# Gated mix of two attentions on one core: four value tiles behind the query tiles, sixteen more maxima units in the front, two-step cycles from step 159

## The chip, the cores and the metric

One core of a Trainium2 chip runs the whole kernel; the other cores are idle. The metric is the device time of one execution in microseconds (us). Engines are named as in the profile: PE is TensorE (PEld its weight loads), DVE is VectorE, ACT is ScalarE, POOL is GpSimd, and SP is SyncE, whose queue (SPq) issues every DMA of this kernel.

## The reference

The input `x` is 2048 tokens of 448 numbers. Two attention layers with 16 heads of 28 read it, and a gate per token mixes their outputs:

```python
g = sigmoid((x * gate_w).sum(-1, keepdims=True))
# A: linear attention with learned feature maps
q, k, v = heads(x @ A_wqkv)
phi_q = cat(softmax(q @ w_phi), softmax(-(q @ w_phi)))      # per head, 28 -> 56
phi_k = the same of k
o_A = phi_q @ (phi_k^T @ v) / (phi_q @ sum(phi_k) + 1e-6)
# B: softmax attention over all 2048 keys
p   = softmax(q' @ k'^T * 28**-0.5);  o_B = p @ v'
out = g * (o_A @ A_wo) + (1 - g) * (o_B @ B_wo)
```

Everything is float32. A precise product is made of passes with split numbers: `fp32r` high parts and low parts (`XH`, `XL`), high times high, high times low, low times high.

## The kernel before, in words

**Two parts.** The front (about the first 330 us) makes queries, keys and values of both layers, does all of layer A, and begins layer B. The back (the loop over `s`, 256 steps) does the softmax attention of B.

**Units and steps of B.** Heads come in 4 groups `g` of 4, and queries in 4 blocks `qb` of 512. A pair `gq = 4 g + qb` has 16 steps, one for every 128 keys. In a step the 4 heads' scores are made (`score_group`, line 965, four `st` tiles of 128 keys x 512 queries), ACT takes the exponentials (line 968), and `values` (line 1069) adds `p` times the values into the tile `pv`. The row maximum of every query, which is subtracted inside the score product, must be known before its pair begins: it is loaded into row 0 of the query stack `qst` (`load_nm`).

**Two ways to find the maxima.** In the front, `mx_unit` takes 128 queries x 2 heads x 1024 keys: four matmuls of 28 rows (line 293) into a bank pair `pmb` and a bank pair `pmd`, one ACT `Relu` over `pmd` (line 296), two DVE sums-with-maximum (line 298). A pair `gq` has 16 units. The first `NF` = 44 units are done in the front, so pairs 0 and 1 and three quarters of pair 2. In the back, `mx_visit` does 128 queries x 4 heads x 512 keys: four matmuls (line 330), one ACT pass (line 334), and three DVE reductions and sums (lines 338 and 341), and one more reduction after every fourth visit (line 344). 212 visits do the rest.

**The cycle of steps.** Up to step `TWO` = 191 every step has a visit, and scores are issued as 5 tiles at an even step and 3 at an odd one ("single steps"). From step 191 scores of two steps are issued together at an odd step (8 tiles), both steps' values follow, and only the even step has a visit ("two-step cycles"). So the visits end at step 234 and the maxima of pair 15 are there for step 240.

**Order of the work.** PE, DVE, ACT and POOL run their instructions in the order in which the program writes them; the DMAs on SP are ordered by the scheduler of the framework, and SP issues them one after the other, so that a DMA whose data isn't ready holds up those behind it.

**The front's long loop** runs over `i` from 0 to 42, with `t = i` (16 token tiles for keys and values of A) and `q = i - 16` (16 query tiles of A). For `t` < 16 an iteration does the key tile (`pk`), its features, and the value tile (`pva`); `tick`, called before each of their matmuls, puts units between them at the places in `pace["at"]`. From `q` = 0 on come the query tile `pq`, its features (maxima and minima on DVE, differences on POOL or DVE, exponentials on ACT), the transposes `pft` (`turn`), the numerators `pn` (`numer`), and from `q` = 11 the output tiles of A, `poa` (`out_a`, `out_a2`). The numerators of a block of 256 queries `tb` are divided in four places: `normalize1` copies them to `oUa` and sends the denominators (`dena`) through a DMA; `normalize2` inverts them on DVE and sends them through memory (`rda`) to all partitions (`rsa`); `normalize3`, three iterations later, multiplies on DVE (line 428); `normalize4`, one iteration later, splits the result, ACT high (line 436) and POOL low (line 437); after that `poa` can begin. At `q` = 18 the first tile `vb` of B's values is opened and `value_b` fills it, one tile of 11 matmuls (`pvb`) per iteration, tiles 0 to 7 at `q` = 18 to 25. From `q` = 11 each iteration has one unit.

**PSUM.** There are 8 banks. In the front's pool `ps` three banks rotate for single tiles (tag `s`), with a fourth taken every fourth time (`turn4`), and two bank pairs (tag `mx`) serve `pmb` and `pmd`. After the long loop the pool is closed and opened again with two single banks and three bank pairs (`psn` = 2, 3): two for `pmb`, one for `pmd`.

**The junction.** After the loop the stacks `qst0`, `kst0` to `kst4`, `qst1` are made: a fill with 0 of 128 x 2048 (line 870) and, for keys, a fill of row 0 with -1 (line 872); `qst0`, `kst0` and `kst1` on DVE, the others on POOL. Then queries, maxima and keys are loaded, and value tiles 8 to 14 are made with the 3 units that are left between them, and tile 15 with the scores of step 0.

Of the kernel before, what the change touches and what calls it, by code (L numbers as in the profile page):

```python
# [17 lines left out]
P = 128  # L18
# [11 lines left out]
NF = 44  # L30
# [10 lines left out]
def gated_mix_kernel(ctx, tc, xT, wqkB, wvB, wvA, wkAT, wqAT, phi, woA, woB,  # L41
# [224 lines left out]

    def mx_unit():
# [27 lines left out]
        rl = rlp.tile([P, 2, 512], F32, tag="rl", name=f"rl{u}", bufs=2 if psn[1] == 3 else 1)  # L295
# [6 lines left out]
        if gq == GM and qt == QM - 1:  # L302
            mx_load(g, c)
        if r == 15:
            mx_reduce(gq)
# [247 lines left out]
    po_of = {}  # L553
# [37 lines left out]
    def out_a(t):  # L591
        tb, tl = divmod(t, 2)
        po_of[t] = po = ps_s(f"poa{t}")
        run(po[:, :D], [x for g in range(NG)
                        for x in out_passes(oTs[tb][g // 2], g % 2 * 256 + tl * P, woA_s[:, :, :, :D], g)])
# [151 lines left out]
    def value_b(t, mid=None):  # L747
        pv = ps_s(f"pvb{t}")
        tok_major(pv, t, wvB_s, D, mid)
        nc.scalar.copy(vb[t // 8][:, t % 8, :, 0:DH], pv[:, :D].rearrange("p (h d) -> p h d", d=DH))  # L750
# [12 lines left out]
    for i in range(2 * NT + 11):  # L763
# [4 lines left out]
        if t < NT and t % 2 == 0:  # L768
            mx_unit()
            passes = (55 if t < NT - 4 else 44) + (4 if t >= 4 else 0)  # L770
            pace["n"] = 4 if t >= 4 else 0
            pace["at"] = [passes // 3, 2 * passes // 3] if t in (4, 6, 8) else [passes // 2]
# [13 lines left out]
        if q == 2:  # L786
# [4 lines left out]
            kvT = kv_copy()  # L791
            turn4.append("")
# [15 lines left out]
        if 0 <= t - 1 < NT - 1:  # L808
            fk[t - 1] = features2(fk[t - 1], f"k{t - 1}")
        if q in (0, 1) or q >= 11:  # L810
            mx_unit()
# [41 lines left out]
        if 0 <= q - NT - 2 < 8:  # L853
            value_b(q - NT - 2)
# [12 lines left out]
    def stack(nm, keys):  # L867
        r = at.tile([P, 4, 512], F32R, name=nm)
        eng = nc.vector if nm in ("qst0", "kst0", "kst1") else nc.gpsimd
        eng.memset(f32(r), 0.0)  # L870
        if keys:
            eng.memset(f32(r[0:1]), -1.0)
        return r
# [17 lines left out]
    def load_k(g, kb):  # L891
        kst_of[(g, kb)] = load_stack(kst[(4 * g + kb) % 5], k_d[g], kb * 512, (0, 1, 0, 1))

    NS = NG * NQ * NT
    TWO = 191
# [81 lines left out]
    ps_s_.close()  # L977
    ps = ps_s_.enter_context(tc.tile_pool(name="psv", bufs=1, space=PSUM, reuse_waits="tile"))
    psn[:] = 2, 3
    turn4.clear()  # L980
# [129 lines left out]
    def finish(gq, s):  # L1110
# [26 lines left out]
        d2, d3, d4 = (3, 8, 9) if s < 216 else (2, 5, 5)  # L1137
# [162 lines left out]
```

## Time and profile before

| what | value |
|---|---|
| three runs | 1008.59 us median, 1005.69 to 1008.81 |
| the profiled execution | 1007.98 us, of which the span of the trace is 1006.2 us |
| busy in the span | PE 997.0, ACT 803.4, DVE 679.2, POOL 237.4 us |
| granted clock of TensorE | 0.998 of full speed |
| DMA | 106.23 MB, 106 GB/s on average |
| the long loop's last part, 266 to 311 us | PE 44.70 of 45, DVE 15.42, ACT 22.09 |
| junction, 311 to 334 us | PE 22.58 of 23, DVE 12.52, POOL 14.52, DMA 0.85 |
| single steps, 396 to 600 us | PE 204.00 of 204, ACT 197.56, DVE 167.14 |
| two-step cycles, 823 to 885 us | PE 62.00 of 62, ACT 61.47, DVE 30.05 |

How to read it: the page gives the share of the span in which each engine was busy, then the same in 40 equal slices, then the chain of work that ended last. The end of a matmul is modelled and matmuls overlap, so PE at 99% says that work lay on it nearly all the time, and not that it couldn't go faster. What a stretch really costs is read from the starts of its instructions in the timeline.

### The profile page before, as it was taken

To read this page: it belongs to the slowest core of one execution; us is meant where nothing else is said; L and a number is where in the kernel's file an instruction comes from. 1 tells how busy PE (TensorE), PEld (TensorE's weight loads), DVE (VectorE), ACT (ScalarE), POOL (GpSimd) and SP (SyncE) were. 2 spreads that over 40 slices of the span, in tenths; PEclk is the share of its full clock that TensorE was granted. 3 is DMA by queue.
4 is the path that set the end of the run, shared out by engine and by line. 5 is a ranking of instruction groups with operands and counts; after the bars stand their busy time and mean duration, and the time that the engine had idled before them with its cause. 6 is when DMAs were issued, how large, how long until landed. Compare 5 with 4: busy or idle time off the path is not lost.

```text
span 1006.2 us, 17986 instructions
## 1 busy us (share of the span) xinstructions
PE 997.0 (99%) x6472; PEld 556.3 (55%) x6472; DVE 679.2 (67%) x1340; ACT 803.4 (80%) x1532; POOL 237.4 (24%) x215
## 2 busy tenths in 40 slices
PE   9999999989999999999999999999999999999998
PEld 8878888868888433333333333333333334455656
DVE  5557766997535688888888888888887874544202
ACT  5445545667743899999999999999999999979682
POOL 1265456687436103111011110101201011001010
PEclk9999999999999999999999999999999999999999
DMA  8976313312235703333532123431324345515131
GB/s 296 313 234 212 118 50 108 113 47 82 92 116 137 158 10 84 83 75 77 120 69 75 44 67 86 102 90 49 90 52 97 81 98 145 147 38 148 60 107 55
DMA packets 67769, 106.23 MB, mean 106 GB/s; under 512 B 18368, under 2 KB 28208, under 8 KB 67680
## 3 DMA queue, kind: packets, MB, share of 16 engines
q1 hardware_dynamic: 67680, 105.08, 38.6%
q8 instruction: 51, 0.84, 0.4%
q14 instruction: 38, 0.31, 0.1%
HBM read 73.21 MB, written 31.45 MB: 104 GB/s over the span
## 4 chain that ended last, share of the span: by engine, by line
PE 77%; DVE 0%; ACT 0%; issue 0%
PE st L965 28%; PE pv L1069 25%; PE pm L330 9%; PE poa L117 4%; PE pob L117 3%; PE pvb L135 2%; PE pvb L117 2%; PE pq L117 1%; PE pmb L293 1%; PE pft L533 1%; PE poL L1107 1%; PE pn L547 1%; PE poL L1177 0%; DVE part L341 0%; PE pr L1162 0%; PE pd L1152 0%
## 5 line engine op out<-in xcount | busy, mean ns | idle before, releaser
L968 ACT ACTIVATE p<-st 128x512 f32<-128x512 f32 x1020 | 529.3, 639 | 25.7 <-PE st L965 25.7
L341 DVE TENSOR_REDUCE part<-pm 128x1 f32<-128x512 f32 x477 | 304.7, 685 | 134.8 <-PE pm L330 134.8
L965 PE MATMUL st<-qst,kst 128*128 128x512 f32 x1020 | 303.1, 423 | 0.4 <-DVE acc L1084 0.4
L1069 PE MATMUL pv<-p,vb 128*32 128x512 f32 x2048 | 266.1, 603 | 0.0
L965 PEld LDWEIGHTS st<-qst,kst 128*128 128x128 f32 x1020 | 167.9, 187 | 99.4 <-ACT p L968 48.9
L334 ACT ACTIVATE rl<-pm 128x512 f32<-128x512 f32 x212 | 132.2, 624 | 15.5 <-PE pm L330 13.4
L330 PEld LDWEIGHTS pm<-kc,qc 28*128 28x128 f32 x848 | 40.5, 181 | 177.8 <-issue 104.8
L428 POOL TENSOR_TENSOR oUb<-oUb,rsb 128x512 f32<-128x512 f32 x15 | 19.4, 1291 | 457.0 <-DMA rsb<-rdb 212.2
L338 DVE CUSTOM_DVE_ANT_0 rl<-pm,rl 128x512 f32<-128x512 f32 x159 | 108.2, 681 | 0.0
L330 PE MATMUL pm<-kc,qc 28*128 28x512 f32 x848 | 107.3, 495 | 0.0
L1069 PEld LDWEIGHTS pv<-p,vb 128*32 128x32 f32 x2048 | 45.4, 108 | 94.1 <-issue 87.4
L298 DVE CUSTOM_DVE_ANT_0 rl<-pmb,rl 128x512 f32<-128x512 f32 x88 | 56.6, 681 | 36.9 <-ACT rl L296 36.9
L117 PE MATMUL pqk<-XH,wB 128*128 128x512 f32 x192 | 59.3, 397 | 0.0
L296 ACT ACTIVATE rl<-pmd 128x1024 f32<-128x1024 f32 x44 | 45.4, 1031 | 8.2 <-PE pmd L293 4.5
L623 ACT CAST ev<-pqk 128x512 fp32r<-128x512 f32 x28 | 16.1, 589 | 38.6 <-PE pqk L117 28.8
L117 PE MATMUL poa<-woA_s,oTa 128*128 128x448 f32 x192 | 44.6, 382 | 0.0
L117 PEld LDWEIGHTS pqk<-XH,wB 128*128 128x128 f32 x192 | 35.4, 188 | 8.5 <-issue 1.5
L1084 DVE SCALAR_TENSOR_TENSOR acc<-pob,gate,acc 128x448 f32<-128x448 f32 x12 | 8.2, 681 | 47.2 <-PE pob L117 47.2
L117 PEld LDWEIGHTS poa<-woA_s,oTa 128*128 128x128 f32 x192 | 35.9, 194 | 6.9 <-issue 4.2
L204 POOL TENSOR_TENSOR kc<-kc,kd 28x512 fp32r<-28x512 f32 x12 | 15.4, 1281 | 101.6 <-DMA kc<-qkd 45.8
L624 DVE TENSOR_TENSOR ev<-pqk,ev 128x512 fp32r<-128x512 f32 x28 | 19.1, 690 | 28.8 <-ACT ev L623 28.7
L135 PE MATMUL pva<-wvA_s,XH 128*128 128x450 f32 x128 | 37.6, 371 | 0.0
(163 smaller groups left out, 1175.8 us busy)
## 6 DMA issues: line engine op xcount, KB each, us to landing
qkd<-ev SPq DMA_DIRECT2D x28, 512.0 KB
qst<-qkd SPq DMA_DIRECT2D x64, 224.0 KB
kst<-qkd SPq DMA_DIRECT2D x64, 224.0 KB
od<-oTb SPq DMA_DIRECT2D x48, 112.0 KB
rsa<-rda SPq DMA_DIRECT2D x8, 512.0 KB
rsb<-rdb SPq DMA_DIRECT2D x15, 256.0 KB
kc<-qkd SPq DMA_DIRECT2D x64, 56.0 KB
gad<-ga SPq DMA_DIRECT2D x16, 224.0 KB
```

Of the source, the lines that this page charges most:

```text
L117: nc.tensor.matmul(dst, l, r, start=i == 0, stop=i == len(todo) - 1)
L135: nc.tensor.matmul(dst[:, :n], l, r, start=i == 0, stop=i == len(todo) - 1, skip_group_check=True)
L296: nc.scalar.activation(rl, pd, AF.Relu)
L298: nc.vector.tensor_tensor_reduce(rl[:, i, :], pb[:, i, :], rl[:, i, :], 1.0, LOWEST, ALU.add, ALU.max, part[:, col + i:col + i + 1])
L330: nc.tensor.matmul(pm[j], mxs[("qc", gq)][js, qt * P:(qt + 1) * P], mxs[("kc", g, kb)][js, :], start=True, stop=True, tile_position=(32 * ...
L334: nc.scalar.activation(rl, pm[kb], AF.Relu if kb < 3 else AF.Copy)
L338: nc.vector.tensor_tensor_reduce(r, pm[j], r, 1.0, LOWEST, ALU.add, ALU.max, part[:, col + j:col + j + 1])
L341: nc.vector.tensor_reduce(part[:, col + j:col + j + 1], pm[j], AX.X, ALU.max)
L428: (nc.gpsimd if n == 1 else nc.vector).tensor_mul(oU, oU, rs)
L965: nc.tensor.matmul(st, kst_of[(gq // NQ, kt // 4)][:, j, (kt % 4) * P:(kt % 4 + 1) * P], qst_of[gq][:, j, :], start=True, stop=True)
L968: nc.scalar.activation(p, st, AF.Exp, scale=SCALE)
L1069: nc.tensor.matmul(pv[32 * j:32 * j + 32, :], vb[kt // 8][:, kt % 8, 4 * g + j, :], pt[j], start=kt == 0, stop=kt == NT - 1, tile_position ...
```

## The change

It has six parts.

1. **Four value tiles earlier.** `value_b(0)` to `value_b(3)` run in the iterations `q` = 7 to 10, right behind the query tile's features. Since `vb` isn't open then, they write into two new tiles `early` (`ve`, 128 x 2 x 512 each), whose columns 28 to 31 POOL fills at `q` = 2. At `q` = 18, when `vb` is opened, two DMAs of 512 KB copy them into it. `value_b(4)` to `(7)` run at `q` = 18 to 21; at `q` = 22 to 25 there is no value tile.
2. **Sixteen more units in the front.** `NF` goes from 44 to 60: pairs 0 to 2 and three quarters of pair 3. `pace` gives two places inside every two key and value tiles, not only at `t` = 4, 6, 8 (5 units more); at `q` = 20 and 21 there is a unit inside the value tile (2 more); 12 units stand at the junction and among value tiles 8 to 14, where there were 3. The first visits then belong to head group 0 for four steps only, and group 1's keys are loaded from the last unit on.
3. **Bank pairs.** The pool `ps` is closed and opened with two single banks and three pairs at `q` = 20, not after the loop. The units' work tile `rl` then comes from the tag `rl2`, which the `early` tiles used.
4. **Fills.** All fills of the stacks are on POOL, with one fill of row 0 for `kst0` alone; `kst1` to `kst4` get their row 0 from `kst0` by a DMA of 8 KB each, in `load_k`.
5. **Two-step cycles from step 159.** `TWO` goes from 191 to 159. There are 196 visits in place of 212, and they still end at step 234.
6. **Distances.** The steps of a pair's division in the back (`d2, d3, d4`) are (2, 5, 5) from step 159, not from 216.

```diff
-NF = 44
+NF = 60
@@ mx_unit
-        rl = rlp.tile([P, 2, 512], F32, tag="rl", name=f"rl{u}", bufs=2 if psn[1] == 3 else 1)
+        rl = rlp.tile([P, 2, 512], F32, tag=rlt[0], name=f"rl{u}", bufs=2 if psn[1] == 3 else 1)
...
             mx_load(g, c)
+            if c == NQ - 1 and qb == NQ - 1:
+                mx_load(g + 1, 0)
@@ out_a
-        po_of[t] = po = ps_s(f"poa{t}")
+        po_of[t] = po = po_next.pop() if po_next else ps_s(f"poa{t}")
@@ value_b
-        pv = ps_s(f"pvb{t}")
+        pv = pv_next.pop() if pv_next else ps_s(f"pvb{t}")
         tok_major(pv, t, wvB_s, D, mid)
-        nc.scalar.copy(vb[t // 8][:, t % 8, :, 0:DH], pv[:, :D].rearrange("p (h d) -> p h d", d=DH))
+        v = early[t // 2][:, t % 2] if t < 4 else vb[t // 8][:, t % 8]
+        nc.scalar.copy(v[:, :, 0:DH], pv[:, :D].rearrange("p (h d) -> p h d", d=DH))
@@ the long loop
-            pace["at"] = [passes // 3, 2 * passes // 3] if t in (4, 6, 8) else [passes // 2]
+            pace["at"] = [passes // 3, 2 * passes // 3] 
...
+            early = [ta.tile([P, 2, 512], F32, tag="rl2", name=f"ve{i}", bufs=2) for i in range(2)]
+            early = [e.rearrange("p t (h d) -> p t h d", d=32) for e in early]
+            for e in early:
+                nc.gpsimd.memset(e[:, :, :, 28:], 0.0)
+                nc.gpsimd.memset(e[:, :, :, 28:29], 1.0)
...
+        if 7 <= q < 11:
+            value_b(q - 7)
+        if q == NT + 4:
+            ps_s_.close()
+            ps = ps_s_.enter_context(tc.tile_pool(name="psv", bufs=1, space=PSUM, reuse_waits="tile"))
+            psn[:] = 2, 3
+            turn4.clear()
+            rlp, rlt[0] = ta, "rl2"
+            pv_next.append(ps_s("pvb_next"))
+            po_next.append(ps_s("poa_next"))
...
             vb = [value_tile(0)]
-        if 0 <= q - NT - 2 < 8:
-            value_b(q - NT - 2)
+            for k, e in enumerate(early):
+                nc.sync.dma_start(vb[0][:, 2 * k:2 * k + 2], e)
+        if 0 <= q - NT - 2 < 4:
+            value_b(q - NT + 2, (lambda i: i == 5 and mx_unit()) if q >= NT + 4 else None)
@@ stack
-        eng = nc.vector if nm in ("qst0", "kst0", "kst1") else nc.gpsimd
-        eng.memset(f32(r), 0.0)
-        if keys:
-            eng.memset(f32(r[0:1]), -1.0)
+        nc.gpsimd.memset(f32(r), 0.0)
+        if nm == "kst0":
+            nc.gpsimd.memset(f32(r[0:1]), -1.0)
@@ load_k
+        n = 4 * g + kb
+        if 0 < n < 5:
+            nc.sync.dma_start(f32(kst[n][0:1]), f32(kst[0][0:1]))
+        kst_of[(g, kb)] = load_stack(kst[n % 5], k_d[g], kb * 512, (0, 1, 0, 1))
...
-    TWO = 191
+    TWO = 159
@@ the junction
-    ps_s_.close()
-    ps = ps_s_.enter_context(tc.tile_pool(name="psv", bufs=1, space=PSUM, reuse_waits="tile"))
-    psn[:] = 2, 3
-    turn4.clear()
+    rlt[0] = "rl"
@@ finish
-        d2, d3, d4 = (3, 8, 9) if s < 216 else (2, 5, 5)
+        d2, d3, d4 = (3, 8, 9) if s < TWO else (2, 5, 5)
```

More of the change, by code (lines that the diff above doesn't have):

```diff
@@ L265, in mx_reduce @@
         mxs["fin"].append(reduce)
+    rlt = ["rl"]
     def mx_unit():
@@ L551, in numer @@
         num[tb] = normalize1(ta, pn, f"a{tb}", 2)
-    po_of = {}
+    po_of, po_next, pv_next = {}, [], []
     def load_woA(b):
@@ L891, in load_k @@
     def load_k(g, kb):
-        kst_of[(g, kb)] = load_stack(kst[(4 * g + kb) % 5], k_d[g], kb * 512, (0, 1, 0, 1))
+        n = 4 * g + kb
+        if 0 < n < 5:
+            nc.sync.dma_start(f32(kst[n][0:1]), f32(kst[0][0:1]))
+        kst_of[(g, kb)] = load_stack(kst[n % 5], k_d[g], kb * 512, (0, 1, 0, 1))
     NS = NG * NQ * NT
-    TWO = 191
+    TWO = 159
     slots = {"n": 0}
```

## The prediction

> **What bounds the kernel now.** I read the page first, for what is full.
>
> ```profile
> PE 997.0 (99%) x6472; PEld 556.3 (55%) x6472; DVE 679.2 (67%) x1340; ACT 803.4 (80%) x1532; POOL 237.4 (24%) x215
> ...
> PE 77%; DVE 0%; ACT 0%; issue 0%
> ```
>
> PE is full and the chain of work lies on it, so the time is the sum of what PE issues and of its few gaps. Next the timeline of PE where the back goes from single steps to two-step cycles (columns: start, duration, engine, line, operation, tiles, count):
>
> ```profile
> 817.11 0.51 PE L330 MATMUL pm<-kc,qc 28*128 28x512 f32 x4
> ...
> 819.44 0.50 PE L330 MATMUL pm<-kc,qc 28*128 28x512 f32 x4
> ...
> 822.28 0.51 PE L330 MATMUL pm<-kc,qc 28*128 28x512 f32 x4
> 822.71 2.48 PE L965 MATMUL st<-qst,kst 128*128 128x512 f32 x8
> ...
> 827.41 2.49 PE L965 MATMUL st<-qst,kst 128*128 128x512 f32 x8
> ...
> 832.12 2.22 PE L965 MATMUL st<-qst,kst 128*128 128x512 f32 x8
> ...
> 836.56 2.21 PE L965 MATMUL st<-qst,kst 128*128 128x512 f32 x8
> ```
>
> From 817.11 to 822.28, two steps with two visits take 5.17 us. After 822.71, two steps with one visit take 4.70 the first time, then 4.44 (832.12 to 836.56). The windows give the means:
>
> ```profile
> 750.50:822.80 72.30, 72.30 (x453) 27.79 (x449) 58.83 (x119) 70.14 (x141) 6.37 (x6) 1.00 0.42 95
> 822.80:858.90 36.10, 36.10 (x225) 16.25 (x226) 17.09 (x34) 35.82 (x74) 3.17 (x3) 1.00 0.52 135
> ```
>
> The first is 14 times 5.16 us, the second 8 times 4.51. ACT is at 97% and 99% in them, so ACT is nearly full too; in the front it isn't. The front's only long gap of PE stands ahead of the first output tile:
>
> ```profile
> 215.75 2.70 DVE L428 TENSOR_TENSOR oUa<-oUa,rsa 128x1024 f32<-128x1024 f32 x1 [0.23 <-DMA rsa<-rda]
> ...
> 217.38 0.50 PE L293 MATMUL pmd<-kp,qp 28*128 28x512 f32 x2
> 218.48 1.14 ACT L436 CAST oTa<-oUa 128x512 fp32r<-128x512 f32 x2 [3.58 <-DVE oUa L428]
> 221.00 1.55 PE L547 MATMUL pn<-fT,KV 56*32 56x256 f32 x32 [3.12 <-ACT fT L536]
> ```
>
> ```profile
> 217.90:221.00 3.10, 0.00 (x1) 0.01 (x1) 2.97 (x5) 2.52 (x5) 1.94 (x2) 1.00 0.23 94
> 221.00:226.20 5.20, 5.20 (x45) 3.69 (x46) 5.13 (x11) 3.72 (x6) 5.20 (x5) 0.67 0.15 46
> ```
>
> In the windows the columns are: stretch, length, then busy time and count of PE, PEld, DVE, ACT and POOL, the granted clock, DMA share and GB/s. DVE, full in this stretch, comes late to the first multiplication (L428); ACT waits for it 3.58 us, and the copies of the transposes behind it on ACT are what PE waits for. Then PE runs 5.2 us at a granted clock of 0.67.
>
> **The change, part by part.**
>
> *Back, from step 159 (gain).* 32 steps, or 16 pairs of steps, go from 5.16 to 4.51 us: 16 x 0.65 = 10.4 us less. Bounds: all at 4.44, 11.5 less; all like the first at 4.70, 7.4 less. The shorter distances put the division's wait (DMA of denominators) on DVE 2 steps after the pair's end, 4.5 us; DVE is busy 17.09 of 36.10 there, so I cost it at nothing.
>
> *Sixteen units in the front (loss).* A unit inside a value tile of the junction, and the same tile without one:
>
> ```profile
> 315.41 0.57 PE L135 MATMUL pvb<-wvB_s,XH 128*128 128x448 f32 x2
> ...
> 316.02 0.97 PE L135 MATMUL pvb<-wvB_s,XH 128*128 128x448 f32 x4
> ...
> 319.26 0.56 PE L135 MATMUL pvb<-wvB_s,XH 128*128 128x448 f32 x2
> 319.75 0.50 PE L293 MATMUL pmb<-kp,qp 28*128 28x512 f32 x2
> ...
> 320.50 0.57 PE L135 MATMUL pvb<-wvB_s,XH 128*128 128x448 f32 x2
> ```
>
> Three passes take 0.61 us without and 1.24 with it, so a unit costs 0.63. All sixteen stand inside tiles: 16 x 0.63 = 10.1 us more. Lower bound 16 x 0.50 = 8.0, the busy time alone. So the units moved pay for themselves and no more; what is left decides. Their ACT and DVE work lies beside PE, if the bank pairs come free in time. It is one pass on ACT and two on DVE each, with a short read behind each of the two; and one unit of the profile that took its way through the engines slowly:
>
> ```profile
> L298 DVE CUSTOM_DVE_ANT_0 rl<-pmb,rl 128x512 f32<-128x512 f32 x88 | 56.6, 681 | 36.9 <-ACT rl L296 36.9
> L296 ACT ACTIVATE rl<-pmd 128x1024 f32<-128x1024 f32 x44 | 45.4, 1031 | 8.2 <-PE pmd L293 4.5
> ...
> 129.60 0.50 PE L293 MATMUL pmb<-kp,qp 28*128 28x512 f32 x2
> ...
> 133.18 0.69 DVE L298 CUSTOM_DVE_ANT_0 rl<-pmb,rl 128x512 f32<-128x512 f32 x1
> ```
>
> From the matmuls to the last read it took 4.3 us. With two pairs the next unit must wait for it. At `t` = 12 to 15 the units now follow each other after 16 passes (3.3 us) and 0.5 of their own, 3.8 us: up to 0.5 us late for each of 5. I take 0.6 us in all, between 0 and 2.5. At the junction there are three pairs, and 12 units need 12 x 2 x 0.68 = 16.4 us of DVE in the 23 us that seven tiles and 12 units take on PE (7 x 2.2 + 12 x 0.63): nothing.
>
> *Four value tiles at `q` = 7 to 10 (gain).* PE's work is the same, 11 matmuls each, only moved. But four times 2.2 us (11 x 0.61 / 3) now lie between DVE's late multiplication and PE's need of it, 9 us in place of a lag of 3.1. The gap goes: 3.1 us, and 5.2 x 0.33 = 1.7 us of slow clock, together 4.8 us less. The value tile's copy now stands ahead of the same ACT work, so I leave 0.3 us at the first numerator behind it. Bounds: 4.8 less to 0, if the wait only moves.
> The Trainium skill (TensorE: Matmul & The Clock Gate, Part 1) says that PE falls to half clock after an idle window of about 3.4 us. By that a gap of 3.1 us would cost no clock and the part be worth 3.1 us; the window above shows 0.67 after 3.10 us, and the measurement decides.
>
> *Copies and later value tiles.* The two copies of 512 KB enter the queue at `q` = 18, beside the last denominators. The last block's way in the profile:
>
> ```profile
> 284.91 1.14 SPq L421 DMA_DIRECT2D rda<-dena  x2
> 287.87 0.55 SPq L422 DMA_DIRECT2D rsa<-rda  x1
> ...
> 297.58 1.23 DVE L428 TENSOR_TENSOR oUa<-oUa,rsa 128x1024 f32<-128x1024 f32 x1 [3.13 <-DMA rsa<-rda]
> ...
> 300.59 2.53 POOL L437 TENSOR_TENSOR oTa<-oUa,oTa 128x512 fp32r<-128x512 f32 x2 [8.46 <-ACT oTa L436]
> 302.63 2.73 PE L117 MATMUL poa<-woA_s,oTa 128*128 128x448 f32 x12
> ```
>
> From `rda` to the end of POOL's split it takes 18.2 us (284.91 to 303.12), and poa14 began after 17.7 without waiting, its last passes alone needing the split's end. In the change, between these places stand poa10 to poa13 (4 x 2.7), value tile 7 (2.2) and five units (5 x 0.6), 16 us, since poa12 to poa14 no longer have a value tile each. So PE waits here some 1 us (bounds 0 and 7, below).
>
> *Bank pairs at `q` = 20.* The reopening costs a wait of 0.72 us for ACT's last read:
>
> ```profile
> 311.42 0.50 PE L293 MATMUL pmb<-kp,qp 28*128 28x512 f32 x2 [0.72 <-ACT ga L599]
> ```
>
> It moves from after poa15 to after value tile 5, and unit 39 or poa9 meets it. With the copy out of the value tile in that bank and a unit between them, I count 0.3 less; bounds: nothing less, and 0.7 less.
>
> *Fills.* DVE loses five fills, POOL has seven and one row:
>
> ```profile
> L870 POOL MEMSET kst<- 128x2048 f32 x3 | 5.5, 1825 | 0.0
> L872 POOL MEMSET kst<- 1x2048 f32 x3 | 5.4, 1801 | 0.2
> ...
> kst<-qkd SPq DMA_DIRECT2D x64, 224.0 KB
> ...
> 334.00:336.00 2.00, 2.00 (x16) 1.10 (x17) 1.48 (x3) 1.98 (x5) 0.00 (x0) 1.00 0.93 186
> ```
>
> Eight times 1.8 is 14.5 us on POOL; `kst0`, third in order, is ready after 5.4 us. Scores begin 23 us after poa15, so it costs nothing. Behind the fills stand the DMAs: one query stack and four key stacks of 4 x 224 KB (4.6 MB), and maxima keys and queries of two groups, some 2 MB, of which the second group's now come at steps 1 to 8. At 186 GB/s that is 35 us from about 8 us after poa15 on; the last piece is needed at step 8, some 45 us after it (23 and 8 x 2.6). Nothing, but it is near. The row copies of `kst1` to `kst4` are four more DMAs of 8 KB, behind a fill that is done before them.
>
> **Sum.** -10.4 + 10.1 - 4.8 + 0.3 + 0.6 + 1.0 - 0.3 = -3.5. The profiled execution took 1007.98 us, which gives 1004.5. It lies 0.6 under the median of the three runs (1008.59).
>
> **The rivals.**
> 1. *The last denominators come late (slower).* The two copies stand in SP's order ahead of the last `dena`; 1 MB at 186 GB/s is 5.6 us. If they push that chain back in full, poa14 waits 1.0 + 5.6 us and 1.7 more for the clock: 8.3 in place of 1.0, so 1011.8. It decides from a delay of 3 to 4 us. For it: in the profile the chain has less slack than a value tile is long. Against: the copies need only the fill of `vb`, and so may be done before the last block's `oUa` is written.
> 2. *The gap moves.* DVE stays behind and the first output tile waits as before: 4.8 us come back, 1009.3, no change. Against: DVE has 9 us more for the same work.
> 3. *The banks bind.* The five close units and the twelve at the junction wait for DVE by the upper bound and 1 us beyond: +3, 1007.5, no change. For it: the 4.3 us against 3.8. Against: a pair waits for DVE only while features stand ahead of the unit there.
> 4. *Key loads late in steps 5 to 8.* A visit waits 3 us for `kc`, 1007.5. For it: the DMA share of 0.93 at that place. Against: by the sum above the last piece lands 2 us before its step, and the others earlier.
>
> **How the numbers follow.** Less than 0.3% (3 us) can't be told from no change. Forecast 0.60; rival 1 0.15; rival 2 0.10; rival 3 0.08; rival 4 0.07. The forecast's own range: from 1000.5 (back at 4.44, 1.1 less; no new wait, 1.9 less; units half-way to their bound, 1.0 less) to 1007.5 (each of the two waits by 1.5 us longer). The forecast is faster by over 0.3% where it comes out at 1005 or less; its middle is barely there, but its gains have firmer rows than its waits, and I give it 0.53 of the 0.60. The other 0.07 and most of rivals 2 to 4 are no change, 0.28; rival 1 and the tails of rivals 2 and 4 are slower, 0.19. The range reaches to rival 1 without its full price: 1000.5 to 1010.5.
>
> **What would show it.** Two-step cycles from step 159 at 4.4 to 4.7 us; no gap of PE ahead of poa0, and the granted clock at 1.00 there; the front longer by about 7 us up to step 1; a wait of about 1 us ahead of or inside poa14. Wrong would be: a wait over 3 us at poa12 to poa15, waits of PE for DVE ahead of units at `t` = 12 to 15, or for a DMA in steps 5 to 8.

## The result, and the profile after

The kernel after takes 1013.0 us (median of 11 runs, 1010.57 to 1015.88) against 1008.02 for the kernel before on the same chip: a ratio of 1.0056, 95% interval 1.0040 to 1.0072. It is slower by 0.56%; forecast were 1004.5 (1000.5 to 1010.5), and faster. In a second measurement (e17 below) the ratio was 1.0063 (1.0041 to 1.0084).

The profiled execution took 1015.46 us, its span is 1013.7 (before: 1006.2). The page's lines that answer to those of before:

```profile
PE 1001.0 (99%) x6472; PEld 560.9 (55%) x6472; DVE 655.7 (65%) x1335; ACT 810.1 (80%) x1532; POOL 240.2 (24%) x220
...
PE 92%; issue 2%; DVE 2%; DMA 1%; POOL 1%; ACT 1%; SPq 1%; POOLq 0%; DVEq 0%; ACTq 0%
```

The two chains can't be compared share by share: before, the chain could be followed back only to the start of PE at 221.00 us, behind its gap, and for these 77% of the span it was PE alone. Now it runs through the whole span, and behind 221 us it has pieces that aren't PE's, among them transfers: `kc<-qkd` for 5.46 us from 361.20, and `kst<-qkd` for 4.42 and 4.87 us from 820.43 and 824.92. PE waits in new places. Where, the timeline of PE of the kernel after shows (start, duration, engine, line, operation, tiles, count, and in brackets the idle time and what ended it):

```profile
298.29 0.50 PE L295 MATMUL pmd<-kp,qp 28*128 28x512 f32 x2 [1.40 <-ACT rl L298]
...
304.87 2.73 PE L117 MATMUL poa<-woA_s,oTa 128*128 128x448 f32 x12
...
308.96 0.68 PE L117 MATMUL poa<-woA_s,oTa 128*128 128x448 f32 x2 [0.92 <-ACT oTa L440]
310.32 3.59 PE L117 MATMUL poa<-woA_s,oTa 128*128 128x448 f32 x10 [0.69 <-POOL oTa L441]
...
366.70 0.82 PE L334 MATMUL pm<-kc,qc 28*128 28x512 f32 x4 [0.71 <-DMA kc<-qkd]
...
829.85 2.04 PE L989 MATMUL st<-qst,kst 128*128 128x512 f32 x4 [1.77 <-DMA kst<-qkd]
```

Three places: the end of the front (a unit's `pmd` bank, then poa14, whose last 10 passes take 3.59 where all 12 of poa13 take 2.73, since the granted clock was at half; the last section shows it), steps 5 to 8 of the back, and the scores of step 192. The wait of 3.12 ahead of poa0 is gone:

```profile
220.56 0.57 PE L117 MATMUL pvb<-wvB_s,XH 128*128 128x448 f32 x2
221.06 1.09 PE L551 MATMUL pn<-fT,KV 56*32 56x256 f32 x32
222.08 1.09 PE L537 MATMUL pft<-ident,feat 128*128 128x128 f32 x8
```

To see where time is won and lost I took from each trace the start of the first `pv` matmul of each step, counted from the kernel's first matmul, and subtracted that of before. These differences are the columns of the table; a difference between two columns is what the stretch between them cost or saved. Step 0 closes the front; the steps from 159 on are the new two-step cycles. Medians are those of the runs, each with the ratio to before.

| run | step 0 | step 16 | step 144 | step 192 | end | median, ratio (95%) |
|---|---|---|---|---|---|---|
| after | 12.35 | 14.75 | 14.84 | 7.38 | 7.34 | 1013.0, 1.0056 (1.0040 to 1.0072) |
| after again (e17) | 12.53 | 17.86 | 17.82 | 10.59 | 10.48 | 1013.87, 1.0063 (1.0041 to 1.0084) |
| e1 tiles alone | 5.86 | 5.89 | 5.97 | 6.04 | 6.11 | 1013.77, 1.0064 (1.0045 to 1.0083) |
| e2 units alone | 21.21 | 21.25 | 21.29 | 14.11 | 13.97 | 1022.77, 1.0150 (1.0124 to 1.0176) |
| e3 writes after loads | 10.25 | 17.76 | 17.78 | 6.85 | 6.68 | 1011.89, 1.0047 (1.0028 to 1.0066) |
| e4 tiles spread | 12.44 | 12.44 | 12.58 | 3.66 | 3.55 | 1012.53, 1.0053 (1.0035 to 1.0071) |
| e5 third `ga` | 13.34 | 16.76 | 16.70 | 9.84 | 9.73 | 1017.05, 1.0092 (1.0070 to 1.0114) |
| e6 copies later | 13.45 | 17.81 | 17.76 | 10.53 | 10.46 | 1017.11, 1.0094 (1.0073 to 1.0115) |
| e7 e1 with three mends | 3.19 | 3.21 | 3.17 | 3.28 | 3.29 | 1011.50, 1.0039 (1.0026 to 1.0051) |
| e8 after with four mends | 16.75 | 18.23 | 18.46 | 7.53 | 7.49 | 1015.56, 1.0075 (1.0050 to 1.0100) |
| e9 copies on GpSimd | 6.73 | 9.93 | 9.91 | 3.26 | 3.47 | 1012.60, 1.0058 (1.0042 to 1.0074) |
| e10 e1, copies on GpSimd | 0.00 | 0.03 | -0.02 | 0.07 | 0.08 | 1009.58, 1.0025 (1.0014 to 1.0037) |
| e11 e9 and queue order | 6.34 | 7.83 | 7.70 | -3.14 | -2.88 | 1006.58, 0.9995 (0.9983 to 1.0007) |
| e12 e10, third `ga` | 1.56 | 1.58 | 1.51 | 1.61 | 1.67 | 1009.78, 1.0023 (1.0013 to 1.0033) |
| e13 e11, query load early | 6.90 | 6.94 | 7.05 | -3.89 | -3.64 | 1004.20, 0.9967 (0.9955 to 0.9979) |
| e14 e10, tiles spread | 0.61 | 0.62 | 0.59 | 0.74 | 0.73 | 1009.50, 1.0019 (1.0006 to 1.0031) |
| e15 e14, third `ga` | 1.18 | 1.23 | 1.31 | 1.30 | 1.28 | 1009.03, 1.0004 (0.9989 to 1.0019) |
| e16 e13, copies by DMA again | 9.48 | 9.47 | 9.49 | -1.43 | -1.50 | 1008.62, 1.0005 (0.9991 to 1.0019) |

The columns come from one profiled execution each, and executions of one kernel differ by several us (the kernel after by 5.3 and 6.8 in its two measurements, the kernel before by 4.5 beside the first), so verdicts go by the medians and the columns say where. The profiled execution of the kernel after was the second longest of its 11, that of e17 the longest of its 6.

### The profile page after: what moved, and what is told of

It is laid out like the page before. It is cut to its first block, busy times and chain, and to the rows that moved or that the text cites. A ratio compares the mean times of both kernels' runs of the same rounds, so it can differ in the third digit from the quotient of the medians.

```text
span 1013.7 us, 17983 instructions
## 1 busy us (share of the span) xinstructions
PE 1001.0 (99%) x6472; PEld 560.9 (55%) x6472; DVE 655.7 (65%) x1335; ACT 810.1 (80%) x1532; POOL 240.2 (24%) x220
## 4 chain that ended last, share of the span: by engine, by line
PE 92%; issue 2%; DVE 2%; DMA 1%; POOL 1%; ACT 1%; SPq 1%; POOLq 0%; DVEq 0%; ACTq 0%
PE st L989 27%; PE pv L1090 24%; PE pm L334 8%; PE pqk L117 6%; PE pk L135 4%; PE pva L135 4%; PE poa L117 3%; PE pob L117 3%; PE pq L117 2%; PE pmb L295 2%; PE pvb L135 2%; PE pft L537 1%; PE pvb L117 1%; PE pqk L690 1%; DMA kst<-qkd 1%
## 5 line engine op out<-in xcount | busy, mean ns | idle before, releaser
L345 DVE TENSOR_REDUCE part<-pm 128x1 f32<-128x512 f32 x441 | 281.9, 686 | 157.5 <-PE pm L334 157.5
L338 ACT ACTIVATE rl<-pm 128x512 f32<-128x512 f32 x196 | 121.7, 621 | 16.5 <-PE pm L334 15.6
L1090 PEld LDWEIGHTS pv<-p,vb 128*32 128x32 f32 x2048 | 48.1, 108 | 96.7 <-issue 90.0
L334 PE MATMUL pm<-kc,qc 28*128 28x512 f32 x784 | 100.3, 495 | 1.2 <-DMA kc<-qkd 0.7
L300 DVE CUSTOM_DVE_ANT_0 rl<-pmb,rl 128x512 f32<-128x512 f32 x120 | 77.1, 680 | 36.9 <-ACT rl L298 36.7
L342 DVE CUSTOM_DVE_ANT_0 rl<-pm,rl 128x512 f32<-128x512 f32 x147 | 100.1, 681 | 0.0
L298 ACT ACTIVATE rl<-pmd 128x1024 f32<-128x1024 f32 x60 | 61.6, 1027 | 13.4 <-PE pmd L295 11.6
L135 PE MATMUL pk<-wkA_s,XH 128*128 128x448 f32 x128 | 37.6, 375 | 0.0
```

The costliest lines, as they stand in the source:

```text
L135: nc.tensor.matmul(dst[:, :n], l, r, start=i == 0, stop=i == len(todo) - 1, skip_group_check=True)
L298: nc.scalar.activation(rl, pd, AF.Relu)
L300: nc.vector.tensor_tensor_reduce(rl[:, i, :], pb[:, i, :], rl[:, i, :], 1.0, LOWEST, ALU.add, ALU.max, part[:, col + i:col + i + 1])
L334: nc.tensor.matmul(pm[j], mxs[("qc", gq)][js, qt * P:(qt + 1) * P], mxs[("kc", g, kb)][js, :], start=True, stop=True, tile_position=(32 * ...
L338: nc.scalar.activation(rl, pm[kb], AF.Relu if kb < 3 else AF.Copy)
L342: nc.vector.tensor_tensor_reduce(r, pm[j], r, 1.0, LOWEST, ALU.add, ALU.max, part[:, col + j:col + j + 1])
```

## The experiments

**The two halves, and two first mends.** My theory after the first look: the saved gap and the faster cycles are real; the loss is made of the three new waits; and the end of the front waits because the last denominators lost the value tiles that covered them.

e1 takes back the units and the cycles; value tiles, bank pairs and fills stay:

```diff
-NF = 60
+NF = 44
-            pace["at"] = [passes // 3, 2 * passes // 3] 
+            pace["at"] = [passes // 3, 2 * passes // 3] if t in (4, 6, 8) else [passes // 2]
-            value_b(q - NT + 2, (lambda i: i == 5 and mx_unit()) if q >= NT + 4 else None)
+            value_b(q - NT + 2, None)
-    TWO = 159
+    TWO = 191
-        d2, d3, d4 = (3, 8, 9) if s < TWO else (2, 5, 5)
+        d2, d3, d4 = (3, 8, 9) if s < 216 else (2, 5, 5)
```

> The kernel after with its 16 units and its two-step cycles taken back (44 units in the front at their old places, two-step cycles from step 191): only the value tiles, the earlier bank pairs and the fills are left. The theory (the gap ahead of poa0 is really saved, -4.8, and the four tiles are then missing behind poa12 to poa15, where the last denominators' chain comes late, +1 to +3): 1004.5 to 1007, against 1008.0 before. The rival that the moved tiles cost as much as they save (the chain late by 4 and more): 1008 or above. The rival that all of the loss is the units': 1003.2. The wait ahead of poa0 is to be gone by every theory.

Measured: 1013.77, so "1008 or above", the rival that the moved tiles cost as much as they save. PE's waits in e1's front (timeline):

```profile
280.75 0.50 PE L295 MATMUL pmb<-kp,qp 28*128 28x512 f32 x2 [1.56 <-ACT ga L603]
...
307.21 0.79 PE L295 MATMUL pmd<-kp,qp 28*128 28x512 f32 x2 [3.66 <-ACT rl L298]
```

The gap ahead of poa0 is gone here too, but behind it e1 loses more than twice what it saves: step 0 comes 5.86 later than before with the same work. The tiles, without the units, make the kernel slower by 0.64%.

e2 is the other half, on the kernel before:

```diff
-NF = 44
+NF = 60
-    TWO = 191
+    TWO = 159
-            pace["at"] = [passes // 3, 2 * passes // 3] if t in (4, 6, 8) else [passes // 2]
+            pace["at"] = [passes // 3, 2 * passes // 3] 
...
             mx_load(g, c)
+            if c == NQ - 1 and qb == NQ - 1:
+                mx_load(g + 1, 0)
...
-        d2, d3, d4 = (3, 8, 9) if s < 216 else (2, 5, 5)
+        d2, d3, d4 = (3, 8, 9) if s < TWO else (2, 5, 5)
```

> The kernel before with the 16 units added to its front and two-step cycles from step 159, and nothing else. The theory (16 units at 0.63 to 0.97 cost 10 to 13; the cycles save 10; new waits in steps 0 to 8 and at step 191 cost about 5): 1013 to 1016. The rival that units and cycles cancel as the prediction had it, and that the loss comes of the moved tiles, banks and fills: 1007.5 to 1009. With e1 this splits the change in two; if the two parts add up, the two differences to before sum to the +5.0 of the whole.

Measured: 1022.77, far outside both. One wait of PE at the junction makes most of it (timeline of e2, DVE and PE):

```profile
315.47 1.76 DVE L872 MEMSET qst<- 128x2048 f32 x1 [0.67 <-PE poa L117]
317.61 1.76 DVE L872 MEMSET kst<- 128x2048 f32 x1 [0.38 <-issue]
319.86 1.76 DVE L874 MEMSET kst<- 1x2048 f32 x1 [0.48 <-DVE kst L872]
322.00 1.76 DVE L872 MEMSET kst<- 128x2048 f32 x1 [0.38 <-issue]
324.24 1.76 DVE L874 MEMSET kst<- 1x2048 f32 x1 [0.48 <-DVE kst L872]
...
327.23 0.79 PE L293 MATMUL pmb<-kp,qp 28*128 28x512 f32 x2 [7.96 <-DVE part L298]
```

Five fills stand on DVE for 10.5 us (315.47 to 326.00), and the units of the junction need DVE's reads. In the kernel before only 3 units stood there. So the halves do not add up (+5.9 and +14.9 against +5.0): the units need the fills off DVE, which is in e1's half. That e1's half needs the units as cover is not shown by these two runs; e9 beside e10 below bears it out.

e3 moves four output writes behind the key loads of the last group:

```diff
-                for j in range(4):
-                    r = (4 * g + j) * DH
-                    nc.sync.dma_start(o_d[r:r + DH, :, qb * 512:(qb + 1) * 512],
-                                      f32(st["o"][32 * j:32 * j + DH]))
+                def f5():
+                    for j in range(4):
+                        r = (4 * g + j) * DH
+                        nc.sync.dma_start(o_d[r:r + DH, :, qb * 512:(qb + 1) * 512],
+                                          f32(st["o"][32 * j:32 * j + DH]))
+
+                if s == 176:
+                    late.setdefault(s + 14, []).append(f5)
+                else:
+                    f5()
```

> The kernel after, with the four output writes of one group (the ones that sat ahead of the last key stacks in SP's queue from 807.8 to 819.9 and waited for GpSimd) issued nine steps later, behind those loads. The theory (queue order: the loads wait behind the writes, and the 1.77 us wait at step 191 with the slow clock behind it costs 2.6): 1010.4, and the two-step region keeps its gain of 9.9 to its end. The rival (the DMA engines' share of 0.97 there is the limit, whatever the order): 1013, the wait stays.

SP's queue in the kernel after, and the scores in the same place of e3 (timelines):

```profile
816.38 3.40 SPq L1151 DMA_DIRECT2D od<-oTb  x4
819.88 1.83 SPq L898 DMA_DIRECT2D kst<-qkd  x4
821.76 0.39 SPq L898 DMA_DIRECT2D qst<-qkd  x1
822.19 2.48 SPq L910 DMA_DIRECT2D qst<-nm  x4
824.92 4.08 SPq L898 DMA_DIRECT2D kst<-qkd  x4
```

```profile
829.80 2.23 PE L989 MATMUL st<-qst,kst 128*128 128x512 f32 x8
834.25 2.50 PE L989 MATMUL st<-qst,kst 128*128 128x512 f32 x8
```

The waits of SP's queue between 770 and 835 in the kernel after (who waited, for what, us in total, times, longest):

```profile
SPq L1151 <- POOL oTb L441: 14.6, 2, 8.6
```

The writes wait 8.6 for POOL's split, with key stacks and the next queries and maxima behind them. In the same stretch the key loads also wait up to 8.8 for buffers that the scores still read, before the edit and after it (8.7 in e3), so that alone does not make them late. With the writes behind the loads no score waits, and from step 144 to 192 the kernel gains 10.9 (17.78 to 6.85) in place of 7.5 (14.84 to 7.38). Queue order it is, not the DMA engines' share. The median, 1011.89, lies between the theory's 1010.4 and the rival's 1013; it went down by 1.1 only, and e3's profile shows why that says little: it lost 7.5 in steps 0 to 16, where the edit changes nothing and the kernel after lost 2.4 once and 5.3 the other time.

e4 spreads value tiles 4 to 7:

```diff
-        if 0 <= q - NT - 2 < 4:
-            value_b(q - NT + 2, (lambda i: i == 5 and mx_unit()) if q >= NT + 4 else None)
+        if q in (NT + 2, NT + 4, NT + 6, NT + 8):
+            value_b(4 + (q - NT - 2) // 2, (lambda i: i == 5 and mx_unit()) if q >= NT + 4 else None)
```

> The kernel after with value tiles 4 to 7 at every second step of the loop (18, 20, 22, 24) and not in a row at 18 to 21, so that poa12 to poa15 have tiles between them again. The theory (those steps were too short for the chain of the last denominators: waits of 0.9 and 0.7 ahead of poa14 and a slower clock behind, 3 in all): 1010, no wait at poa14. The rival (the chain itself starts late, behind the two copies in SP's queue): poa14 waits as before, 1013. If the steps 18 to 22 become too short instead, a wait shows ahead of poa11 to poa13.

Measured: 1012.53, front as long as before the edit (12.44). poa14 waits no more, but other waits stand for it:

```profile
284.63 0.50 PE L295 MATMUL pmb<-kp,qp 28*128 28x512 f32 x2 [2.92 <-ACT ga L603]
298.31 0.67 PE L135 MATMUL pvb<-wvB_s,XH 128*128 128x448 f32 x2 [1.46 <-ACT ga L603]
```

Cover moved along the end of the front only moves the wait: something ahead of it is late. In these traces it is ACT, held at `ga` by a DMA (kernel after, timeline of ACT):

```profile
283.28 0.64 ACT L603 ACTIVATE ga<-poa,gate 128x448 f32<-128x448 f32 x1 [2.77 <-DMA gad<-ga]
...
296.69 0.63 ACT L603 ACTIVATE ga<-poa,gate 128x448 f32<-128x448 f32 x1 [4.63 <-DMA gad<-ga]
```

**What holds the DMAs at the end of the front.** e5 gives `ga` a third tile (`bufs=2` to `bufs=3`), e6 issues the copies of the early tiles at `q` = 24:

> The kernel after with a third ga tile (three where there were two), so that ScalarE's product behind a poa need not wait for the second last product's write to DRAM, which stands in SP's queue behind the chain of the denominators. The theory (in the end of the front it is ScalarE, held by that write, 4.63 ahead of ga(10), that keeps TensorE: pmd waits 1.40, and everything behind is late): the ga waits go, the wait at pmd with them, poa14's 0.9 and 0.7 may stay or grow: 1.5 to 3 less, 1010 to 1011.5. The rival (only the chain of the last denominators counts; ga is late because of it, not the reverse): the wait moves to poa12 or poa14 and the time stays at 1013.

> The kernel after with the two copies of the early value tiles issued six steps later (step 24 of the loop, behind the last rsa), so that nothing of them stands in SP's queue ahead of the last denominators. Rival 1 of the prediction (the copies make the last dena late): the last dena is issued some 1.5 to 3 earlier against the unit beside it, poa14's wait goes, 1010 to 1011. The theory (the chain is long in itself, its DMAs wait for VectorE and for one another, and the two copies take only 1.4 of the queue): 0 to 1 less, 1012 to 1013.

e5: 1017.05. The `ga` and `pmd` waits are gone, but poa14 waits 3.13 for ACT's split and 0.68 for POOL's: the denominators' chain was late by as much. The wait moved to poa14, as the rival had it, but the time lies outside both forecasts, and why it is 4 above the kernel after stays open. e6: 1017.11, outside both forecasts too, and here the edit did not do what I wrote of it: the scheduler put the first copy where it was (276.96) and the second 5 us later (283.66), still ahead of the last `dena` (284.28). The run shows a tie that I had overlooked (e6, timelines of SP and ACT):

```profile
276.96 0.54 SPq L879 DMA_DIRECT2D vb<-ve  x1
...
283.66 0.53 SPq L879 DMA_DIRECT2D vb<-ve  x1
284.28 1.30 SPq L414 DMA_DIRECT2D dena<-oUa  x2
...
293.07 1.02 ACT L298 ACTIVATE rl<-pmd 128x1024 f32<-128x1024 f32 x1 [5.24 <-DMA vb<-ve]
```

The units' `rl` tiles at the end of the front have the same two buffers (`rl2`) as the early value tiles, so a unit cannot pass before a copy has read its buffer. A late copy stops the units.

e7 is e1 and e8 is the kernel after, each with third `ga`, copies at `q` = 24 and spread tiles; e8 has e3's edit too:

> The kernel of e1 (value tiles, bank pairs and fills, but neither units nor two-step cycles) with a third ga tile, the two copies six steps later, and value tiles 4 to 7 at steps 18, 20, 22, 24 of the loop. The theory (of e1's waits, 1.6 + 0.7 + 3.7 and the slow matmuls behind them, nearly all come of ScalarE held by ga's writes in the steps that lost their value tiles): the 4.8 saved ahead of poa0 are then kept, 1003 to 1005.5, faster than before by 0.25 to 0.5%. The rival (the work that was moved is cover that the end of the front needs, wherever it is put: each us saved ahead of poa0 comes back as a wait for the denominators' chain): 1007 to 1010, with waits at poa10 to poa15.

> The kernel after with all four mends: third ga tile, copies later, value tiles spread, output writes behind the key stacks. By the sum of the parts (after 1013; -3 to -4 for the end of the front, -2.6 to -3.5 for step 191; steps 0 to 8 as they fall, 0 to 2.4): 1005.5 to 1008, about the kernel before. If the moved tiles need their cover back (the rival of e7): 1009 to 1011.

1011.5 and 1015.56, outside the ranges of theory and rival alike. Both carry e6's flaw: PE waits 4.49 and 6.10 at a `pmd` for ACT's `rl`, which waits for `vb<-ve` (6.34 and 6.48). e8's back, with e3's edit, gains the full 10.9 again.

**The copies without DMA.** Three waits (`ga` writes, the last denominators, the `rl` buffers) had the copies in common. e9 makes them in SBUF on POOL, in the kernel after; e10 in e1:

```diff
-                nc.sync.dma_start(vb[0][:, 2 * k:2 * k + 2], e)
+                nc.gpsimd.tensor_copy(vb[0][:, 2 * k:2 * k + 2], e)
```

> The kernel after with the two copies of the early value tiles made by GpSimd in SBUF and not by two DMAs in SP's queue. The earlier runs show ScalarE's units held by those DMAs (waits of 6.3 and 5.2 for them where they were issued later) and by the ga writes that stand between them (4.63 in the kernel after). The theory (the copies by DMA, 512 KB each, are what makes the end of the front late: they hold the ga writes, the last denominators and the unit tiles that share their buffers): the waits at pmd43 and poa14 go, step 0 starts 3 to 4.5 earlier, 1008.5 to 1010. The rival (the chain of denominators is late by itself, for want of the moved tiles): less than 1 saved, 1012 to 1013, poa14 still waits. A second rival (GpSimd's copies, two of some 2.5 between its splits of oTa, make the splits late): a wait for GpSimd's oTa at poa10 to poa12.

> The kernel of e1 (value tiles, bank pairs, fills; no units, no two-step cycles) with the copies on GpSimd. e1 lost 9.9 in waits and slow matmuls between 276 and 312 and saved 4.8 ahead of poa0. The theory: those waits go but for 0 to 2, and the saving stands: 1003.5 to 1006, faster than before. The rival (moved cover): 1008 to 1011.

The windows (stretch, length, busy time and count of PE, PEld, DVE, ACT, POOL, then clock, DMA share, GB/s) of the kernel after and of e9:

```profile
276.00:284.00 8.00, 8.00 (x69) 6.29 (x67) 2.37 (x5) 3.46 (x6) 1.19 (x3) 1.00 0.68 203
...
292.00:300.00 8.00, 6.60 (x33) 4.87 (x32) 3.95 (x11) 3.15 (x6) 0.00 (x0) 1.00 0.31 104
...
308.00:316.00 8.00, 6.39 (x27) 4.65 (x24) 2.99 (x10) 4.25 (x6) 2.52 (x2) 0.79 0.14 52
```

```profile
276.00:284.00 8.00, 8.00 (x71) 6.13 (x69) 2.54 (x5) 3.19 (x6) 3.14 (x5) 1.00 0.27 83
...
292.00:300.00 8.00, 8.00 (x44) 5.96 (x43) 5.09 (x14) 4.91 (x8) 1.66 (x2) 1.00 0.31 108
...
308.00:316.00 8.00, 8.00 (x45) 5.50 (x44) 4.46 (x15) 4.66 (x6) 1.39 (x3) 1.00 0.35 105
```

The DMA share between 276 and 284 falls from 0.68 to 0.27, and PE is full to the end, at full clock. POOL's copies cost 2.02 there:

```profile
277.24 2.02 POOL L874 COPY vb<-ve 128x1024 f32<-128x1024 f32 x2
```

Step 0 of e9 comes 6.73 later than before, 5.6 sooner than in the kernel after. Yet e9's median (1012.6) is hardly lower: in its profile the back lost 3.2 in steps 0 to 16 and gained only 6.7 by step 192. By its number the rival came (1012 to 1013), by its trace the theory, and e9's profiled execution is the shortest of its 6 where that of the kernel after is a long one. So the copies were a cause in one trace, and not shown by the medians. e10 came down to 1009.58 from e1's 1013.77, but not to the 1003.5 to 1006 expected: 2.10 at a `pmd` and a slow poa14 are left, where e9, with the units, has no such waits.

e11 adds the queue's order in the back: e3's edit, and two key stacks moved away from the shallow loads of the second group:

```diff
-        if t in (8, 12):
-            load_k(0, t // 12)
+        if t in (8, 12, 14):
+            load_k(0, (t - 8) // 3)
-            if s in (0, 3):
-                load_k(0, 2 + s // 3)
+            if s == 6:
+                load_k(0, 3)
```

> The kernel of e9 with the output writes behind the key stacks (e3's edit), and the third and fourth key stacks of the first group loaded one step before the back (in place of step 0) and at step 6 (in place of step 3), so that the shallow key and query loads for the second group do not stand behind them in SP's queue. The theory (queue order makes the waits of steps 5 and 8, 1.5 to 7.5 in the runs so far, and that of step 191): both are gone, the back gains 9.5 to 10.5 against before, 1003.5 to 1007. The rival for the early steps (the loads come late whatever stands ahead, since they wait for their buffers): the waits of 0.7 to 2.5 at steps 5 and 8 stay, 1006 to 1009.

1006.58, within both ranges. The wait for `kc` at step 8 and that at step 192 are gone, the cycles gain 10.8 (7.70 to -3.14); 1.5 stays at step 5, for a query load (`qc`). e13 moves that load:

```diff
             if r == 0:
                 mx_query(gq)
+            if r == 8:
+                mx_query(gq + 1)
```

> The kernel of e11 with the shallow query load for the second group's first block issued in the ninth of the last twelve units, and not in the second visit of the back. The theory (the load stands late in SP's queue, behind a key stack): the wait at step 5 goes, and with it 1.4 of the back's start: 1005 to 1006, below before by 0.2 to 0.3%. The rival (the early load only puts another one late): the wait moves to a kc load at steps 5 to 8, 1006.5.

1004.2, ratio 0.9967 (0.9955 to 0.9979): faster than both kernels, and below the 1005 to 1006 of its theory. No step waits for a load, and its front is 6.90 longer, where the prediction's terms sum to 6.9.

**The copies again, by medians.** e16 is e13 with the copies by DMA as in the kernel after; e17 is the kernel after unchanged:

> The kernel of e13 with the two copies of the early value tiles by DMA in SP's queue again, as in the kernel after, and nothing else changed. The theory (these copies make the end of the front late by 4 to 5.6): 1008 to 1010 against e13's 1004.2, with waits at pmd43 or poa14. The rival (they cost little over many executions; the loss of the kernel after is the queue in the back): 1004 to 1005.5.

> The kernel after, unchanged, for a second profiled execution. By the theory it has again waits at the end of the front (pmd or poa14, 3 to 6 in all with the slow matmuls behind), in steps 5 to 8 (0 to 7), and at step 192 (about 2 to 4); median 1012 to 1014.

e16: 1008.62, e13: 1004.2, so the DMA copies cost 4.4 in the medians here, and 4.2 from e10 to e1; from e9 to the kernel after it was only 0.4 (1.3 to e17). e16's back is that of e13 (-10.92 and -10.94 from step 144 to 192), and PE's waits are at the end of the front (timeline):

```profile
297.33 0.50 PE L297 MATMUL pmd<-kp,qp 28*128 28x512 f32 x2 [0.53 <-ACT rl L300]
...
307.50 0.67 PE L117 MATMUL poa<-woA_s,oTa 128*128 128x448 f32 x2 [0.42 <-ACT oTa L442]
```

e17 has the same three places as the first profile, with 5.3 in steps 0 to 16 and 7.2 gained by step 192. e16 differs from the kernel after only in the order of loads and writes at the start of the back and ahead of step 192; that is worth 4.4 to 5.3 in the medians (1013.0 and 1013.87 to 1008.62), and 8.4 once the copies are on POOL (e9 to e13). So the two don't simply add: mended together they are worth 8.8 (1013.0 to 1004.2), the copies mended alone 0.4 to 1.3, the order alone 4.4 to 5.3. Why the copies count for so little while the order is bad is not shown. e16's profiled execution (1006.61) is one of its short ones, so its front in the table shows less of the copies than the medians do.

**Can the tiles do without the units?** e12 gives e10 a third `ga`; e14 gives e10 e4's spread tiles; e15 has both:

> The kernel of e10 with a third ga tile too. If a ga wait is left in e10, it goes here: 0 to 2 less than e10, 1003 to 1005. If the chain of the last denominators is what is left, the same as e10 with the wait at poa12 or poa14.

> The kernel of e10 (value tiles, bank pairs, fills, copies on GpSimd) with value tiles 4 to 7 at steps 18, 20, 22, 24 of the loop. The theory (what is left in e10 is the chain of the last denominators, which is covered when tiles stand between poa11 and poa15): 3.5 to 5 less than e10's 1009.6, 1004.5 to 1006, faster than before. The rival (steps 18 to 22 become too short for the denominators before the last, and the wait moves there): 1008 to 1010.

> The kernel of e14 with a third ga tile. The theory (e14's two ga waits, 1.38 and 2.85 with some slow matmuls behind, are the last): 1004.5 to 1006, faster than before by 0.2 to 0.35%, about the 4.8 saved ahead of poa0. The rival (each cover taken from the end of the front shows the next wait in the chain of writes and denominators): 1007 to 1009.5, with a wait for oTa or oUa at poa10 to poa15.

1009.78, 1009.50 and 1009.03: e14 and e15 within the ranges of their rivals, e12 as long as e10 with the wait at poa14. e12 waits 3.38 at poa14 for ACT's split, e14 1.38 and 2.85 for `ga` writes, e15 1.49 and 2.36 for a `ga` that stands on ACT behind a split, which waits for DVE's multiplication and that for the `rsa` DMA:

```profile
301.46 1.23 DVE L432 TENSOR_TENSOR oUa<-oUa,rsa 128x1024 f32<-128x1024 f32 x1 [5.18 <-DMA rsa<-rda]
```

Without the units, in all the places tried, each cover put in one place uncovers the denominators' chain in another; the four tiles alone keep none of their 4.8. Which of the chain's DMAs would have to be faster was not tried.

## Why the prediction was wrong

By its own terms, from the traces above:

| term of the sum | forecast | measured |
|---|---|---|
| 16 pairs of steps in two-step cycles | -10.4 (-11.5 to -7.4) | -10.9 where no load waits (e3, e11, e13); -7.5 and -7.2 in the kernel after |
| gap ahead of poa0 with its slow clock | -4.8 | -4.8 in the profiled execution: the query tile behind the fourth value tile starts 13.29 later than before, the next, past the gap, 8.49 |
| units, bank pairs, first numerator, reopening | 10.1 + 0.6 + 0.3 - 0.3 | front +6.90 in e13; all the front's terms, the gap's -4.8 and 1.0 for the wait at poa14 among them, sum to 6.9 |
| copies and later value tiles, wait at poa14 | 1.0 (0 to 7) | about 5.5 in the profile of after (12.35 - 6.90); 4.4 in the medians (e16 - e13) |
| key, query and row loads | 0, "near" | 2.4 and 5.3 in steps 0 to 16 |
| division in two-step cycles | 0 | 3.5 at step 192 (-7.46 against -10.94): 1.77 of wait, and 1.7 of half clock behind it |

The gains were right, and so was the price of the units (of the five that stand close, those of the tile pairs that begin at `t` = 12 and 14 moved the start of what follows by 0.97 and 0.95, the other three by 0.6 each: 0.7 of bank waits, forecast 0.6; rival 3 did not come). e13 has the change's work with its waits taken out and takes 1004.2. That its front agrees to 0.1 is partly luck: it has no wait at poa14, for which the sum held 1.0, so the other terms came out 1.0 dearer than forecast. Three steps failed, all on SP's queue.

"Copies and later value tiles" is the mis-sized term. The mechanism and the bounds (0 to 7) were right, the value taken was not. Rival 1 named the mechanism with 1011.8, and I gave it 0.15 for the reason that the copies "may be done before the last block's `oUa` is written". They were issued before it, at 277.28 and 278.49; but 1 MB keeps the DMA engines busy behind that (0.68 over 8 us), `ga` writes stand between and behind the copies, and ACT, which must wait for those writes, is the one that frees `pmd`. I had asked only when the copies start, and had looked at one of the queue's customers. SP's queue in the kernel after (timeline):

```profile
277.28 0.54 SPq L874 DMA_DIRECT2D vb<-ve  x1
277.87 0.58 SPq L604 DMA_DIRECT2D gad<-ga  x1
278.49 0.89 SPq L874 DMA_DIRECT2D vb<-ve  x1
...
280.05 3.47 SPq L414 DMA_DIRECT2D dena<-oUa  x2
```

It was not one wait of 6.6 at poa14, as the rival had it, but several small ones (1.40, 0.92, 0.69) with a slow clock behind the last. The value 1.0 was loosely read besides: the prediction's own 17.7 less 16 is 1.7.

"Nothing, but it is near" summed the loads of the back's start as bytes over 186 GB/s and compared the end. Its margin was thinner than it says: 23 and 8 x 2.6 are 43.8 and not 45, which leaves 0.8 and not 2. The sum may hold; the order did not: the shallow loads that step 5 to 8 need stood behind key stacks for steps 8 and 12. Rival 4 had the place, with 0.07.

In the back the prediction followed the division to DVE and stopped. Its other end, the four output writes that wait on SP for POOL's split, was moved closer to the loads of the last group, and no rival named it. e3 shows that the writes ahead of the loads are the cause; no run took the shorter distances back alone.

The queue's order of the changed steps, with what each DMA waits for, was the view to write out, as it was for PE. Whether it would have shown all three in advance is not tested.

## What to carry to other kernels

When steps get shorter or work moves, write down the order of the one DMA queue around each moved step, with what each transfer waits for and who stands behind it; a transfer that waits for a late engine must stand behind the loads with due times, and here that order was worth 4.4 to 5.3 us. Copies inside SBUF belonged on an engine with time to spare (2.02 us on POOL here) and not in a queue that carries a latency chain (4.4 us on the kernel, once the order was mended). And work that fills one gap of PE may be the cover of another: ask of each moved tile what waited behind it in its old place.

## What the hardware showed that I had not expected

The granted clock falls after gaps shorter than the 3.1 us of the first profile, and what it costs does not depend on the gap's length. Windows laid end to end around the two drops of the kernel after (the first behind the waits of 0.92 and 0.69, the second behind that of 1.77):

```profile
307.55:310.96 3.41, 1.80 (x10) 1.07 (x10) 1.92 (x6) 2.59 (x4) 1.98 (x2) 1.00 0.04 17
310.96:314.37 3.41, 3.41 (x13) 2.36 (x11) 1.26 (x4) 0.37 (x1) 0.55 (x1) 0.50 0.14 50
314.37:317.79 3.42, 3.42 (x21) 2.57 (x18) 1.73 (x6) 1.77 (x3) 0.00 (x0) 1.00 0.44 134
...
826.38:829.79 3.41, 1.70 (x12) 0.86 (x8) 1.89 (x4) 3.11 (x7) 0.00 (x0) 1.00 0.95 180
829.79:833.20 3.41, 3.35 (x12) 1.56 (x16) 0.00 (x0) 2.06 (x4) 0.00 (x0) 0.50 0.65 131
833.20:836.62 3.42, 3.42 (x23) 1.36 (x15) 2.02 (x4) 1.76 (x4) 0.00 (x0) 1.00 0.00 0
```

Each time PE sat idle 1.6 to 1.7 us of a stretch of 3.41, and the next 3.41 us ran at half clock: 1.7 us lost. e15's wait of 2.36 was followed by the same 3.41 us (305.43 to 308.84), so a longer wait cost no more clock; where the second stretch was idle as well, as in e7, the low clock lasted 6.83. The two drops above start 518.83 us apart, which is 152 times 3.413, and in e1, e2, e5, e6 and e17, too, the drops lie whole multiples of 3.413 apart. So the stretches seem to follow a fixed grid, and a wait counts by what falls into one of them. The 2.92 us wait of e4 (at 284.63, shown above) is divided by such a border and left the clock alone:

```profile
279.98:283.40 3.42, 1.72 (x9) 1.25 (x7) 0.52 (x2) 0.24 (x1) 0.00 (x0) 1.00 0.96 240
283.40:286.81 3.41, 2.18 (x13) 1.81 (x14) 1.70 (x2) 2.17 (x4) 0.00 (x0) 1.00 0.27 87
286.81:290.22 3.41, 3.41 (x19) 2.67 (x18) 0.84 (x4) 2.01 (x4) 2.55 (x2) 1.00 0.24 81
```

How much idle time in a stretch it takes is not settled by these traces: 1.56 in e1 was enough, 1.7 in e4 and 1.6 in e2 were not, and the ends of PE's work are modelled. The Trainium skill (TensorE: Matmul & The Clock Gate, Part 1) puts the half clock behind at least one idle window of about 3.4 us. The length of the low stretches, 3.41 us, agrees with that; the idle time ahead of them, as little as 1.56, does not.

The same kernel can meet the drop in one execution and not in the next. Of the 22 executions of the kernel before that ran beside e13, the five with a mean granted clock of 1.000 took 1005.05 us in the median and the other 17 took 1008.20; all of e13's ran at 1.000, so part of its gain is clock.
